# A fused attention and two-layer feed-forward kernel: the order of gates and blocks at two stage changes

## The chip, the cores and the metric

The kernel runs on one core of a Trainium2 chip. The metric is the device time of one execution in microseconds (us); of several runs the median counts. Five engines work side by side, each through its own queue in order: PE (matrix products; its weight loads are shown as PEld), DVE (vector), ACT (scalar functions), POOL (GpSimd) and SP, which issues the transfers.

## What is computed

```python
def reference(q, k, v, ...):
    x = attention(q, k, v, bias from w1, b1, w2)   # 2 x 576 rows, 8 heads of 64, float32
    x = x.reshape(1152, 512)
    h = x @ moe_w_in                               # layer 1: 512 -> 2048
    x = (h / (1 + exp(-1.702 * h))) @ moe_w_out    # gate of layer 1, 2048 -> 512
    h = x @ moe2_w_in                              # layer 2
    P = a0 + a1*h + a2*h**2 + a3*h**3
    Q = 1 + |b0|*|h| + |b1|*h**2
    return (P / (Q + 1e-6)) @ moe2_w_out
```

## The kernel before

**Precision.** Every large product is made from float32 numbers that are split into a high and a low part (hi, lo), as three products: hi by hi, weight lo by hi, weight hi by lo. ACT casts the high part, and POOL or DVE subtracts it from the number to get the low one.

**Attention** runs over 30 steps `s` (head pair, batch, block of 128 rows) and five more, s = 30 to 34, that drain it. The probabilities of step s - 3 are turned by PE (`transposes`, L295) into two PSUM banks `pt`, which ACT copies to SBUF as `PT` (`evacuate`, L354) in the next pass of the loop. Each bank must be copied before the next transposes write it. `values` (L370, L373) multiplies `PT` by v into `xt`, and `values_out` (L390, ACT) and `values_lo` (L395, DVE) make of it the input `xhi`, `xlo` of layer 1. In the passes s = 31, 32 and 33 the first three hidden blocks of layer 1 are computed beside that.

**The two layers.** The 1152 rows are three chunks of 384, and the 2048 hidden columns are 16 blocks `k`. One turn `n` of the main loop issues on PE one hidden block (`hidden`, L483, 12 products into one of two PSUM buffers `hps`) and usually one output block (`out1`, L564, of layer 1, 12 products; `out2`, L571, of layer 2, 9 products) into the banks `acc`. In this text H0 to H47 are the hidden blocks of layer 1, G0, G1, ... those of layer 2; o0 to o47 and p0, p1, ... are the output blocks of the two layers.

- The gate of layer 1 (`gelu`) is a sigmoid on ACT (L501), a product on DVE (L502, which is the last reader of `hps`), and `parts`: a cast on ACT (L492) and a subtraction on POOL (L495). `ghi` and `glo` have two buffers each.
- The gate of layer 2 (`rational`) is a pipeline over three turns. In one turn it issues for the newest block G(m): L527 to L529 on ACT, L541 and L545 on DVE (L545 is the last reader of `hps`), L542 and L544 on POOL; for G(m-1): L524 and L525 on ACT, L535 and L536 on DVE; for G(m-2): L521 on ACT, L531 on DVE and `parts`. L524 needs another function table than the sigmoid, so an ACT_TABLE_LOAD stands where ACT changes between them. Up to turn 51, L521 and L525 write one PSUM buffer, `es`; from turn 52 L521 writes the bank `acc3`.
- Chunk 2 of layer 2 comes first. The last output blocks of layer 1 belong to chunk 0: after o47, DVE adds the four `acc` banks to earlier partial sums (`input2_sum`, L824). The first output block p0 of layer 2 writes the same banks, so it waits for L824. ACT and POOL split those sums (L829, L830) in the four turns after it.
- Weights come as 64-bit numbers, one half block per transfer. `conv` turns them into float32: L445 on ACT, L446, L451 and L461 on DVE; `split` then makes the two parts (L471 ACT, L472 POOL). L446 writes the PSUM tile `top` while `M.second` is false, and the SBUF tile `tmp` when it is true. A half block of layer 2 goes to where the same block of layer 1 lay, once that is read for the last time. Halves still missing at the change of layer are converted one in every second turn, between the instructions of the rational gate. The last is the output weight of block 15, needed by p15 in turn 67.

Everything is written in the order in which it is issued; no scheduler moves anything. Before the change the order of the blocks at the change of layer is a list:

```python
    turn = [*range(N1 - 2), N1, N1 - 2, N1 + 1, N1 - 1, *range(N1 + 2, len(seq))]   # N1 = 48
    pos = {m: n for n, m in enumerate(turn)}
    ...
        while todo and n >= (pos[todo[0]] + L1 if todo[0] < N1 else todo[0] + L2):  # L1, L2 = 2, 4
```

So G0 stands ahead of H46 and G1 ahead of H47, and an output block is issued two turns (layer 1) or four (layer 2) after its hidden block.

Of the kernel before, what the change touches and what calls it, by code (L numbers as in the profile page):

```python
# [17 lines left out]
NF = 16  # L18
# [4 lines left out]
L1, L2 = 2, 4  # L23
# [551 lines left out]
def attention_moe_moe(tc, t):  # L575
    nc = tc.nc
    new = tc.alloc_tile_pool
    A, M = Attention(tc, t), Moe(tc, t)
# [44 lines left out]
    def beat():  # L623
        i = beats[0]
        beats[0] += 1
        if i >= 41:
            return
        if i == 2:
            A.bias_setup2()
        if 3 <= i < 39:  # L630
            A.bias_out(A.rows[i - 3])
        if 2 <= i < 38:
            A.bias_matmul(A.rows[i - 2])
        if i < 36:
            A.bias_hidden(A.rows[i])
        if i in (10, 17, 24, 31, 39):
            A.bias_load(0, QORDER[(10, 17, 24, 31, 39).index(i)])
        if i in (3, 10):
            A.new_parts(i // 10)
            A.q_high(i // 10)  # L640
        if i in (5, 8, 12, 15):
            A.q_low(i // 10, 0 if i in (8, 15) else 320, 320 if i in (8, 15) else 640)
        if i in (6, 13):
            A.k_high(i // 10)
        if i in (7, 14):
            A.k_low(i // 10)
        if i in (21, 26, 34):
            A.load_v((21, 26, 34).index(i))
        if i in (14, 16, 18, 22):
            A.load_qk(2, (14, 16, 18, 22).index(i))  # L650
        if i == 7:
            nc.vector.memset(small[:, 2:3], -1.5)
            nc.scalar.activation(out=M.pb, in_=ab[:, 4:6], func=AF.Abs)

    n = len(A.steps)
    nj = [0]

    def conv(now=True):
        M.conv(nj[0])
        nj[0] += 1  # L660
        if now:
            M.split()

    pv, hq, due = [], [], []
    A.pv = pv
    g, nh = {}, 0
    for s in range(n + TLAG + 2):
        prep = []
        while s <= 10 and beats[0] < FIRST[s]:
            beat()  # L670
        if s < n:
            hp, b, qc = A.steps[s]
            pb = 2 * hp + b
            i = QORDER.index(qc)
            A.tails(s - TLAG)
            A.scores(s)

            prep = [(2, s - 3)] if s <= 10 else [(s // 5 + 1, s % 5)] if s >= 15 else [(3, s - 10)]
            if s == 11:
                prep.insert(0, (3, 0))  # L680
            if prep[0][0] > 7:
                prep = []
            for x, part in prep:
                if part == 0:
                    A.new_parts(x)
        else:
            A.values_out()
            A.values_lo()
            A.tails(s - TLAG)
        if s == n:  # L690
            A.ps.release()
            M.hs = new(name="hs", bufs=1, space=PSUM, side="right", reuse_waits="tile")
            op.release()
            gp = M.gp = new(name="gate", bufs=1, side="right", reuse_waits="tile")
            mid = new(name="wmid", bufs=1, side="right", reuse_waits="tile")
            for k in range(NEARLY, NMID):
                M.W[k] = mid.tile([128, 4, 512], F32R, name=f"w{k}")
        if s - n in (2, 3):
            g[len(g)] = M.gelu(hq.pop(0))
        if s < 10:  # L700
            beat()
        if s == 10:
            A.xp.release()
            A.xp = new(name="xt", bufs=1, space=PSUM, reuse_waits="tile")
        for piece in (('ea', 'to', 'qh', 'eb', 'ql', 'kh', 'xa', 'su', 'cv', 'pv', 'tr', 'xb', 'no', 'vo', 'kl', 'vl') if s < 12 else ('ea', 'vo', 'to', 'pv', 'eb', 'qh', 'ql', 'kh', 'xa', 'tr', 'xb', 'su', 'no', 'vl', 'cv', 'kl')):
            if piece == 'ea':
                A.evacuate(0)
            elif piece == 'eb':
                A.evacuate(1)
            elif piece == 'su':  # L710
                A.sums(s - 1)
            elif piece == 'to':
                A.tails_out(s - TLAG)
            elif piece == 'vo':
                A.values_out()
            elif piece == 'vl':
                A.values_lo()
            elif piece == 'qh':
                for x, part in prep:
                    if part == 0:  # L720
                        A.q_high(x)
            elif piece == 'kh':
                for x, part in prep:
                    if part == 1:
                        A.k_high(x)
            elif piece == 'kl':
                for x, part in prep:
                    if part == 2:
                        A.k_low(x)
            elif piece == 'ql':  # L730
                for x, part in prep:
                    if part in (1, 3):
                        A.q_low(x, 320 if part == 1 else 0, 640 if part == 1 else 320)
            elif piece == 'xa':
                A.exps(s, 0)
            elif piece == 'xb':
                A.exps(s, 1)
            elif piece == 'no':
                A.normalise(s - 1)
            elif piece == 'tr':  # L740
                A.transposes(s - TLAG)
            elif piece == 'pv':
                for _ in range(5 if s >= n or len(pv) > 5 else 2 if pv and pv[0][1] == 0 else 3):
                    if pv and s >= 10:
                        A.values(*pv.pop(0))
                if s == n + TLAG + 1 and 1:
                    A.values_out()
                    A.values_lo()
            elif piece == 'cv':
                for _ in range(n - s in (3, 7, 12, 17, 21) if s < n else (0, 3, 0, 2, 0)[s - n]):  # L750
                    conv()
        if s < n:
            if s == 10:
                A.load_qk(3)

            if s:
                h, o, c = A.steps[s - 1]
                if h < 3 and (h, 1 - o, c) in A.steps[:s - 1]:
                    due.append((h + 1, c))
            while due and (s in (3, 4) or s >= 10):  # L760
                A.bias_load(*due.pop(0))
            if pb > 1 and i == 1:
                A.load_qk(pb + 2)
            if pb > 2 and i == 1:
                A.load_v(pb)
        if s == 10:
            bp.release()
        if s == n - 25:
            pp.release()
            rp = M.rp = new(name="raw", bufs=1, side="right", reuse_waits="tile")  # L770
            wp = new(name="wearly", bufs=1, side="right", reuse_waits="tile")
            for k in range(NEARLY):
                M.W[k] = wp.tile([128, 4, 512], F32R, name=f"w{k}")

        if s == n - 24:
            for j in range(3):
                M.fetch(j)
        if s - n in (1, 2, 3):
            hq.append(M.hidden(0, nh))
            nh += 1  # L780
# [20 lines left out]
    seq = [(0, c, k) for c in range(NC) for k in range(HF)]  # L801
    seq += [(0, c, k) for c in range(NC)[::-1] for k in range(HF, NF)]
    seq += [(1, c, k) for c in range(NC)[::-1] for k in range(NF)]
    N1 = NC * NF

    turn = [*range(N1 - 2), N1, N1 - 2, N1 + 1, N1 - 1, *range(N1 + 2, len(seq))]
    pos = {m: n for n, m in enumerate(turn)}
    freed = {k: max(pos[n] for n in range(N1) if seq[n][2] == k) for k in range(NF)}
    acc, ng, later, hr = {}, len(g), [], []
    gq = list(range(N1, len(seq)))  # L810
    todo = list(range(len(seq)))
# [18 lines left out]
        nc.gpsimd.tensor_tensor(out=lo, in0=p, in1=hi.bitcast(F32), op=ALU.subtract)  # L830

    for n in range(nh, len(seq) + L2):
        l, c, k = seq[turn[n]] if n < len(seq) else (2, 0, 0)
        M.second = n >= N1 - 2
        if l < 2:
            (hr if l else hq).append(M.hidden(c, k))
        fs = []
        for i in range(2):
            j = nj[0]
            if j < 33:  # L840
                go = i == 0 or n < 6
            elif j < 65:
                go = freed[M.order[j - 1][1]] + L1 * M.order[j - 1][2] < n
                go = go and (n < N1 and (i == 0 or n >= 40 and n % 2 == 0) or n >= N1 + 2 and n % 2 == 0 and i == 0)
            else:
                go = False
            if go and n >= N1:
                fs = M.convs(j)
                nj[0] += 1
            elif go:  # L850
                conv(False)
            if n < N1:
                M.split()
            if i == 0 and n <= len(seq) and ng <= turn[n - 1] < N1:
                g[turn[n - 1]] = M.gelu(hq.pop(0))
        if hr or n >= len(seq):
            r = M.rational(hr.pop(0) if hr else None, n < N1 + 4, fs)
            if r:
# [1 line left out]
        M.split()  # L860
        if later:
            input2_parts()
        while todo and n >= (pos[todo[0]] + L1 if todo[0] < N1 else todo[0] + L2):
            m = todo.pop(0)
            l, c, k = seq[m]
            first = k == 0 or l == 0 and c < 2 and k == HF
# [104 lines left out]
```

## Time and profile before

| | us |
|---|---|
| median of 3 runs (612.31 to 613.96) | 613.54 |
| the profiled execution, its own time | 613.64 |
| its span, first to last instruction | 611.6 |
| PE busy in the span | 575.5 |
| ACT busy | 444.4 |
| DVE busy | 430.0 |
| POOL busy | 393.1 |

The span has four stages: attention with its bias (0 to about 190), layer 1 (to about 400), layer 2 (to about 607), and the last outputs. The table counts work over all of them; a change at a stage boundary is judged by the rows around that boundary. Times in the rows are us from the start of the span. A timeline row gives the start, the duration of the group, engine, line, operation, output and inputs, the count, and in brackets the idle time of the engine just before it with the instruction that ended it.

### The profile page before, as it was taken

Reading aid. Unit: us, or ns where it says so; the run is one execution under the profiler, and the core shown is the slowest. Engines: PE = TensorE matmul, PEld = TensorE weight load, DVE = VectorE, ACT = ScalarE, POOL = GpSimd, SP = SyncE. Lnnn points to the kernel's source line nnn. Section 1 sums busy time; section 2 is a strip of 40 time slices with the busy share of each in tenths; the row PEclk is TensorE's granted clock in tenths of the full one; section 3 lists DMA queues with packets and bytes.
Section 4 is the critical chain, followed back from the end, with each engine's and each line's share of the span. In section 5 each row is a group of like instructions: output and inputs, shape, how many; then the busy total and the mean of one; then the engine's idle time right before and its main releaser. Section 6 shows DMA issues by size and latency. Waiting matters only on the chain. (4 is left out here: it accounts for less than half of the span.)

```text
span 611.6 us, 11023 instructions
## 1 busy us (share of the span) xinstructions
PE 575.5 (94%) x3805; PEld 482.6 (79%) x3805; DVE 430.0 (70%) x922; ACT 444.4 (73%) x928; POOL 393.1 (64%) x466
## 2 busy tenths in 40 slices
PE   6987999999987999999999999979999999999997
PEld 2243466666656899999999999968998998998995
DVE  7989765888874886657554528868998666666663
ACT  7978777898885665546444526688999888788783
POOL 5967656788763675546553536957998566565563
PEclk9989999999998999999999999997999999999999
DMA  5788853826214563525432314511200100001001
GB/s 173 209 265 280 232 211 104 299 83 243 61 36 138 168 195 124 170 75 167 138 112 95 104 36 138 158 48 35 71 0 2 51 2 1 1 1 52 2 1 51
DMA packets 23912, 66.25 MB, mean 108 GB/s; under 512 B 2481, under 2 KB 3377, under 8 KB 23857
## 3 DMA queue, kind: packets, MB, share of 16 engines
q1 hardware_dynamic: 23712, 65.43, 33.8%
q8 instruction: 30, 0.49, 0.3%
q14 instruction: 26, 0.20, 0.1%
q10 hardware_dynamic: 144, 0.13, 0.1%
HBM read 52.30 MB, written 13.25 MB: 107 GB/s over the span
## 5 line engine op out<-in xcount | busy, mean ns | idle before, releaser
L483 PE MATMUL hps<-xhi,w 128*128 128x384 f32 x768 | 152.6, 340 | 2.3 <-DVE part L545 1.0
L483 PEld LDWEIGHTS hps<-xhi,w 128*128 128x128 f32 x768 | 137.9, 190 | 8.0 <-DVE sg L502 1.5
L472 POOL TENSOR_TENSOR w<-tmp,w 128x512 fp32r<-128x512 f32 x64 | 86.7, 1354 | 37.4 <-ACT w L471 31.6
L495 POOL TENSOR_TENSOR glo<-sg,ghi 128x384 fp32r<-128x384 f32 x48 | 49.2, 1025 | 57.7 <-PE acc L564 37.4
L483 PE MATMUL hps<-xlo,w 128*128 128x384 f32 x384 | 82.6, 336 | 0.0
L571 PE MATMUL acc<-w,ghi 128*128 128x512 f32 x288 | 77.2, 398 | 3.3 <-DVE part L824 3.3
L253 POOL TENSOR_SCALAR p<-p,mn 128x512 f32<-128x512 f32 x72 | 55.2, 777 | 37.8 <-ACT p L240 26.3
L564 PE MATMUL acc<-ghi,w 128*128 128x384 f32 x384 | 78.3, 334 | 0.0
L240 ACT ACTIVATE p<-p,mn 128x576 f32<-128x576 f32 x72 | 55.6, 773 | 20.1 <-DVE mn L236 18.1
L483 PEld LDWEIGHTS hps<-xlo,w 128*128 128x128 f32 x384 | 68.5, 189 | 0.0
L564 PEld LDWEIGHTS acc<-ghi,w 128*128 128x128 f32 x384 | 67.6, 188 | 0.0
L542 POOL TENSOR_SCALAR ra<-ra,small 128x384 f32<-128x384 f32 x48 | 28.2, 588 | 56.3 <-ACT ra L527 56.3
L571 PEld LDWEIGHTS acc<-w,ghi 128*128 128x128 f32 x288 | 54.1, 190 | 12.4 <-issue 3.6
L502 DVE TENSOR_TENSOR sg<-hps,sg 128x384 f32<-128x384 f32 x48 | 26.8, 558 | 52.0 <-ACT sg L501 52.0
L236 DVE CUSTOM_DVE_ANT_0 p<-wide,bt 128x576 f32<-128x576 f32 x72 | 52.3, 751 | 2.3 <-PE wide L215 2.1
L492 ACT CAST ghi<-sg 128x384 fp32r<-128x384 f32 x48 | 24.8, 517 | 38.7 <-DVE sg L502 19.9
L544 POOL TENSOR_TENSOR ra<-ra,part 128x384 f32<-128x384 f32 x48 | 49.8, 1038 | 4.0
L445 ACT ACTIVATE up<-raw 128x512 int32<-128x512 uint32 x59 | 37.9, 642 | 19.9 <-DVE tmp L461 15.9
L215 PE MATMUL wide<-k,q 64*128 64x288 f32 (+1 forms) x432 | 45.9, 313 | 2.5 <-ACT st L142 2.0
L564 PE MATMUL acc<-glo,w 128*128 128x384 f32 x192 | 45.0, 334 | 0.0
L501 ACT ACTIVATE sg<-hps 128x384 f32<-128x384 f32 x48 | 23.4, 488 | 28.3 <-PE hps L483 28.3
L571 PE MATMUL acc<-w,glo 128*128 128x512 f32 x144 | 43.1, 397 | 0.0
(112 smaller groups left out, 1187.6 us busy)
## 6 DMA issues: line engine op xcount, KB each, us to landing
raw<-win SPq DMA_DIRECT2D x32, 512.0 KB, 3.5
raw<-wout SPq DMA_DIRECT2D x32, 512.0 KB, 3.5
bias_all<-st SPq DMA_DIRECT2D x36, 295.5 KB, 3.8
bt<-bias_all SPq DMA_DIRECT2D x16, 576.0 KB, 6.0
qk<-qk SPq DMA_DIRECT2D x7, 608.0 KB, 5.3
v<-v SPq DMA_DIRECT2D x8, 320.0 KB, 5.0
out<-o SPq DMA_DIRECT2D x8, 256.0 KB, 2.2
bt<-bias_all SPq DMA_DIRECT2D x8, 144.0 KB, 3.4
```

Of the source, the lines that this page charges most:

```text
L215: nc.tensor.matmul(ps[:, half, 0:288], q[p, x, 128 * qc:128 * qc + 128], k[p, y, 288 * half:288 * half + 288], start=(i == 0), stop=(i == ...
L236: nc.vector.tensor_tensor_reduce(out=pv.rearrange("p (x j) -> p x j", x=2), in0=ps[:, :, 0:288], in1=self.bt[qc][:, a, :].rearrange("p (x ...
L240: nc.scalar.activation(out=pv, in_=pv, func=AF.Exp, bias=mn[:, a:a + 1], scale=-1.0, accum_out=mn[:, 2 + a:3 + a])
L253: nc.gpsimd.tensor_scalar(out=p[:, a, 0:512], in0=p[:, a, 0:512], scalar1=r, scalar2=1.0, op0=ALU.mult, op1=ALU.mult)
L445: nc.scalar.activation(out=self.up[j].bitcast(I32), in_=lo, func=AF.Copy, scale=2.0 ** -29)
L472: nc.gpsimd.tensor_tensor(out=w[:, 2 * o + 1, :], in0=val, in1=w[:, 2 * o, :].bitcast(F32), op=ALU.subtract)
L483: nc.tensor.matmul(ps[:, 0:CH], w[:, wi, 128 * d:128 * d + 128], xx[:, d, :], start=(i == 0 and d == 0), stop=(i == 2 and d == 3))
L495: nc.gpsimd.tensor_tensor(out=glo[:], in0=g, in1=ghi[:].bitcast(F32), op=ALU.subtract)
L542: nc.gpsimd.tensor_scalar(out=t0[0][:], in0=t0[0][:], scalar1=self.pb[:, 1:2], scalar2=1.000001, op0=ALU.mult, op1=ALU.add)
L544: nc.gpsimd.tensor_tensor(out=t0[0][:], in0=t0[0][:], in1=t0[1][:], op=ALU.add)
L564: nc.tensor.matmul(acc[e][:, 0:CH], w[:, wi, 128 * e:128 * e + 128], g[gi][:], start=(first and i == 0), stop=(last and i == 2))
L571: nc.tensor.matmul(acc[e][:], g[gi][:, 128 * e:128 * e + 128], w[:, wi, :], start=(first and i == 0), stop=(last and i == 2))
```

## The change

Two edits. In the drain of attention, the gate of a layer-1 block is issued at the place `cv`, behind that pass's copies of probabilities (L354), and no longer ahead of them. At the change of layer the list is gone: all hidden blocks of layer 1 come first, then those of layer 2; `due` gives the turn of each output block, with o46 in turn 49 and o47 in turn 51. With it, `M.second` turns true at turn 48, where it did at 46, and the conversions of the second layer's weights resume at turn 52, where they did at 50.

```diff
-        if s - n in (2, 3):
-            g[len(g)] = M.gelu(hq.pop(0))
         if s < 10:
             beat()
...
             elif piece == 'cv':
+                if s - n in (2, 3):
+                    g[len(g)] = M.gelu(hq.pop(0))
                 for _ in range(n - s in (3, 7, 12, 17, 21) if s < n else (0, 3, 0, 2, 0)[s - n]):
                     conv()
...
-    turn = [*range(N1 - 2), N1, N1 - 2, N1 + 1, N1 - 1, *range(N1 + 2, len(seq))]
-    pos = {m: n for n, m in enumerate(turn)}
-    freed = {k: max(pos[n] for n in range(N1) if seq[n][2] == k) for k in range(NF)}
+
+    due = [m + L1 + (m - N1 + 3 if m > N1 - 3 else 0) if m < N1 else m + L2 for m in range(len(seq))]
+    freed = {k: max(due[n] - L1 for n in range(N1) if seq[n][2] == k) for k in range(NF)}
...
-        l, c, k = seq[turn[n]] if n < len(seq) else (2, 0, 0)
-        M.second = n >= N1 - 2
+        l, c, k = seq[n] if n < len(seq) else (2, 0, 0)
+        M.second = l > 0
...
-                go = go and (n < N1 and (i == 0 or n >= 40 and n % 2 == 0) or n >= N1 + 2 and n % 2 == 0 and i == 0)
+                go = go and (n < N1 and (i == 0 or n >= 40 and n % 2 == 0) or n >= N1 + 4 and n % 2 == 0 and i == 0)
...
-            if i == 0 and n <= len(seq) and ng <= turn[n - 1] < N1:
-                g[turn[n - 1]] = M.gelu(hq.pop(0))
+            if i == 0 and ng <= n - 1 < N1:
+                g[n - 1] = M.gelu(hq.pop(0))
...
-        while todo and n >= (pos[todo[0]] + L1 if todo[0] < N1 else todo[0] + L2):
+        while todo and n >= due[todo[0]]:
```

What moves on the engines is shown at three places. First ACT at the end of attention, passes s = 32 to 33; `PT` is the copy of the turned probabilities, `sg` and `ghi` the gates of H0 and H1, `xhi` the input of layer 1:

```order
+L354 COPY PT<-pt 128x8x64 x2
 L501 ACT_TABLE_LOAD
 L501 ACTIVATE sg<-hps 128x384
 L492 CAST ghi<-sg 128x384
-L354 COPY PT<-pt 128x8x64 x2
 L390 CAST xhi_103<-xt 128x192
 L390 CAST xhi_105<-xt 128x64 x2
-L501 ACTIVATE sg<-hps 128x384
-L492 CAST ghi<-sg 128x384
-L354 COPY PT<-pt 128x8x64 x2
+L354 COPY PT<-pt 128x8x64 x2
+L501 ACTIVATE sg<-hps 128x384
```

Each pair of copies moves ahead of one gate; the number of instructions stays the same.

Second the change of layer, on PE and on ACT. On PE, `hps<-xhi_101` with w_2977 and w_2978 is H46 and H47; with `xhi_105`, w_1324 and w_1325 it is G0 and G1; `acc` with w_2975 and w_2976 is o44 and o45. Before:

```order
L483 MATMUL hps<-xhi_105,w_1324 128x384 x8
L483 MATMUL hps<-xlo_106,w_1324 128x384 x4
L564 MATMUL acc<-ghi,w_2975 128x384 x8
L564 MATMUL acc<-glo,w_2975 128x384 x4
L483 MATMUL hps<-xhi_101,w_2977 128x384 x8
L483 MATMUL hps<-xlo_102,w_2977 128x384 x4
L564 MATMUL acc<-ghi,w_2976 128x384 x8
L564 MATMUL acc<-glo,w_2976 128x384 x4
L483 MATMUL hps<-xhi_105,w_1325 128x384 x8
L483 MATMUL hps<-xlo_106,w_1325 128x384 x4
L483 MATMUL hps<-xhi_101,w_2978 128x384 x8
L483 MATMUL hps<-xlo_102,w_2978 128x384 x4
```

Now:

```order
L483 MATMUL hps<-xhi_101,w_2977 128x384 x8
L483 MATMUL hps<-xlo_102,w_2977 128x384 x4
L564 MATMUL acc<-ghi,w_2975 128x384 x8
L564 MATMUL acc<-glo,w_2975 128x384 x4
L483 MATMUL hps<-xhi_101,w_2978 128x384 x8
L483 MATMUL hps<-xlo_102,w_2978 128x384 x4
L564 MATMUL acc<-ghi,w_2976 128x384 x8
L564 MATMUL acc<-glo,w_2976 128x384 x4
L483 MATMUL hps<-xhi_105,w_1324 128x384 x8
L483 MATMUL hps<-xlo_106,w_1324 128x384 x4
L483 MATMUL hps<-xhi_105,w_1325 128x384 x8
L483 MATMUL hps<-xlo_106,w_1325 128x384 x4
```

PE's sequence was G0 o44 H46 o45 G1 H47 o46 and is H46 o44 H47 o45 G0 G1 o46; from there on it is the same as before: G2, G3, o47, G4, p0. On ACT, in the same place, the gate of H47 (the second L501 here) comes ahead of the whole rational gate, and of three table loads one is left:

```order
-L527 ACTIVATE ra<-hps 128x384
-L528 ACTIVATE part_2980<-hps,cst 128x384
-L529 ACTIVATE part_2980<-hps,cst 128x384
 L445 ACTIVATE up<-raw 128x512
 L471 CAST w_2973<-tmp 128x512
 L501 ACTIVATE sg<-hps 128x384
 L492 CAST ghi<-sg 128x384
+L501 ACTIVATE sg<-hps 128x384
+L492 CAST ghi<-sg 128x384
+L527 ACTIVATE ra<-hps 128x384
+L528 ACTIVATE part_2980<-hps,cst 128x384
+L529 ACTIVATE part_2980<-hps,cst 128x384
```

Third POOL at the last weight half of layer 2, w_2978 (block 15); each group L542, L544, L495 is one turn:

```order
 L542 TENSOR_SCALAR ra<-ra,small 128x384
 L544 TENSOR_TENSOR ra<-ra,part_2980 128x384
-L495 TENSOR_TENSOR glo<-ra,ghi 128x384
+L495 TENSOR_TENSOR glo<-part_2980,ghi 128x384
 L472 TENSOR_TENSOR w_2978<-tmp,w_2978 128x512
-L542 TENSOR_SCALAR ra<-ra,small 128x384
-L544 TENSOR_TENSOR ra<-ra,part_2980 128x384
-L495 TENSOR_TENSOR glo<-part_2980,ghi 128x384
-L542 TENSOR_SCALAR ra<-ra,small 128x384
-L544 TENSOR_TENSOR ra<-ra,part_2980 128x384
-L495 TENSOR_TENSOR glo<-part_2980,ghi 128x384
```

Its split moves two turns later, from turn 64 to turn 66.

## Rows read from the trace of the kernel before

**Rows 1.** Windows: busy time of each engine, granted clock (PEclk), DMA share, GB/s.

```profile
260.00:280.00 20.00, 20.00 (x118) 20.00 (x117) 12.12 (x21) 10.65 (x21) 11.00 (x10) 1.00 0.36 106
410.00:420.00 10.00, 6.74 (x21) 5.58 (x20) 8.29 (x17) 6.85 (x15) 5.82 (x7) 0.66 0.18 54
```

**Rows 2.** Timeline of PE, end of attention and start of layer 1.

```profile
193.19 0.27 PE L295 MATMUL pt<-cst,p 64*128 64x64 f32 x1 [3.09 <-ACT PT L354]
...
194.32 2.50 PE L483 MATMUL hps<-xhi,w 128*128 128x384 f32 x8
...
197.90 1.74 PE L483 MATMUL hps<-xhi,w 128*128 128x384 f32 x8
...
222.16 1.66 PE L483 MATMUL hps<-xhi,w 128*128 128x384 f32 x8
```

**Rows 3.** Timeline of ACT, end of attention.

```profile
189.73 1.28 ACT L501 ACT_TABLE_LOAD   x1
...
192.14 0.51 ACT L492 CAST ghi<-sg 128x384 fp32r<-128x384 f32 x1 [0.62 <-DVE sg L502]
192.56 1.07 ACT L354 COPY PT<-pt 128x512 f32<-128x512 f32 x2
193.51 0.56 ACT L390 CAST xhi<-xt 128x192 fp32r<-128x192 f32 x3
198.14 0.49 ACT L501 ACTIVATE sg<-hps 128x384 f32<-128x384 f32 x1 [4.06 <-PE hps L483]
```

**Rows 4.** Timeline of DVE, start of layer 1.

```profile
198.66 0.56 DVE L502 TENSOR_TENSOR sg<-hps,sg 128x384 f32<-128x384 f32 x1 [3.94 <-ACT sg L501]
...
216.54 0.56 DVE L502 TENSOR_TENSOR sg<-hps,sg 128x384 f32<-128x384 f32 x1 [0.24 <-ACT sg L501]
...
221.55 0.56 DVE L502 TENSOR_TENSOR sg<-hps,sg 128x384 f32<-128x384 f32 x1 [0.24 <-ACT sg L501]
```

**Rows 5.** Timeline of PE, change of layer.

```profile
385.54 1.55 PE L483 MATMUL hps<-xhi,w 128*128 128x384 f32 x8
...
414.18 1.19 PE L571 MATMUL acc<-w,ghi 128*128 128x512 f32 x2 [3.26 <-DVE part L824]
...
423.26 1.57 PE L483 MATMUL hps<-xhi,w 128*128 128x384 f32 x8
...
427.44 1.57 PE L483 MATMUL hps<-xhi,w 128*128 128x384 f32 x8
```

**Rows 6.** Timeline of ACT, change of layer.

```profile
396.20 1.28 ACT L524 ACT_TABLE_LOAD   x1
397.50 0.53 ACT L524 ACTIVATE part<-ra 128x384 f32<-128x384 f32 x1
...
410.82 0.47 ACT L527 ACTIVATE ra<-hps 128x384 f32<-128x384 f32 x1
...
415.46 0.59 ACT L521 ACTIVATE sq<-ra,small 128x384 f32<-128x384 f32 x1 [2.73 <-DVE part L824]
```

**Rows 7.** Timeline of DVE, change of layer.

```profile
413.48 1.95 DVE L824 TENSOR_TENSOR part<-acc,part 128x384 f32<-128x384 f32 x4
```

**Rows 8.** Timeline of ACT, first chunk of layer 2: L527 of five blocks.

```profile
439.29 0.48 ACT L527 ACTIVATE ra<-hps 128x384 f32<-128x384 f32 x1
...
442.94 0.48 ACT L527 ACTIVATE ra<-hps 128x384 f32<-128x384 f32 x1
...
447.34 0.48 ACT L527 ACTIVATE ra<-hps 128x384 f32<-128x384 f32 x1
...
463.46 0.48 ACT L527 ACTIVATE ra<-hps 128x384 f32<-128x384 f32 x1
...
467.43 0.49 ACT L527 ACTIVATE ra<-hps 128x384 f32<-128x384 f32 x1 [0.31 <-PE hps L483]
```

**Rows 9.** Timeline of POOL, the split of the last weight half, turn 64.

```profile
470.65 1.29 POOL L472 TENSOR_TENSOR w<-tmp,w 128x512 fp32r<-128x512 f32 x1
```

**Rows 10.** Timeline of PE, p15 in turn 67.

```profile
479.79 1.09 PE L571 MATMUL acc<-w,ghi 128*128 128x512 f32 x4
```

## The prediction

> **What bounds the kernel now.** I read the windows first. From about 230 to 376 us PE is busy in the whole of each window at full clock, as in the first row of [rows 1]: there, time can only move if PE's stage starts earlier or ends later. The second row is the exception in the two layers: at the change of layer PE worked 6.74 of 10 us, at a mean clock of 0.66. So two places remain, and I read the timelines of the engines around each.
>
> At the end of attention PE stands 3.09 us before the last transposes, waiting for ACT's copies of `PT` [rows 2]. ACT has them queued behind the first gate: table load at 189.73, sigmoid, a wait for DVE, the cast at 192.14, and only then the copies at 192.56 [rows 3]. H1 after it takes from 194.32 to 197.90 [rows 2], 3.6 us for a block that takes 2.1 later on, so the standstill costs clock too.
>
> At the change of layer the longest standstill is 3.26 us [rows 5]. It ends with L824 on DVE, which frees the output banks [rows 7]. From p0 at 414.18 to G6 at 423.26 three blocks take 9.08 us; two blocks take 4.18 at full clock (423.26 to 427.44) [rows 5], so three should take 6.27. That is 2.8 us lost to the half clock.
>
> **The change part by part.**
>
> *Gate behind copies.* Nothing is added or taken away on any engine; two pairs of copies and two gates change places on ACT. The first copies come where the table load stood, 189.73 instead of 192.56: 2.83 earlier, and PE's transposes with them, from 193.19 to about 190.4. The load follows at 189.73 + 0.95 = 190.7 (0.95 is what the copies take until the next instruction starts, 192.56 to 193.51). From load to cast it is 2.41 as now (189.73 to 192.14), so the cast comes at 193.1. After it come `xhi` (0.42 behind the cast, then about 0.5) and the second copies (0.95), and the sigmoid of H1 starts at about 195.0 instead of 198.14 [rows 2, 3]. H1 itself is done by then: transposes done at 191.5 (194.32 less 2.83), plus 2.1, or 3.6 if the clock is low. So ACT and DVE gain 3.1 us, and PE could gain up to 5.
>
> What decides is who sets the pace next. From the gate at 198.66 on, DVE converts weights between the gates, two halves a turn at first, and a turn takes 5.0 us on it (216.54 to 221.55) against 4.2 on PE. The hidden block at 222.16 starts the moment the gate of the block two before it is done (221.55 + 0.56) [rows 2, 4]. PE's extra lead is therefore spent in front of `hps`, and what reaches 222 is DVE's gain, **3.1 us**. The bounds are 0, if this chain does not start earlier, and PE's 5. The stage after it is full on PE [rows 1], so it carries the gain whole.
>
> *Order at the change of layer.* PE's work is the same. G0 moves from 385.54 to four blocks later, 385.54 + 4 x 2.09 = 393.9, ending at 396.0 [rows 5]. Before that, ACT and DVE have only gates and conversions of layer 1, and two table loads drop out. ACT can take G0 up as soon as it is done, with H47's gate behind it.
>
> From there the length of the chain to L824 decides. It runs through L527 of G0, G1, G2 and G3, one step each. The trace of before has no such steps without gates of layer 1 in them; the nearest are those of the first chunk, where ACT is nearly packed too: 439.29 to 442.94, 3.65 without a conversion, and 442.94 to 447.34, 4.40 with one [rows 8]. No conversion stands in turns 48 to 51 now, so I take 3.65, with a little for the `es` buffer that L521 and L525 share: 3.7. The one table load left lies in the first step, which has no L521 and no `parts` of an older block; it costs 1.30 (396.20 to 397.50, the next instruction starting at once) [rows 6], little more than what it stands in for. Three steps are 11.1, so L527 of G3 comes at 407.2. From L527 to L824 it was 2.66 (410.82 to 413.48), from L824 to p0 0.70 [rows 5 to 7]: L824 at 409.9 and p0 at 410.6 instead of 414.18, **3.6 earlier**. With steps of 4.40 it would be 1.5 earlier. PE's wait for p0 becomes about 1.6 us.
>
> The Trainium skill ("ScalarE: Activation LUTs", What ACT_TABLE_LOAD costs) gives a switch as 1.283 us and a drain of 1.38. The row shows the load alone, 1.28. By the page the one load that still stands on each of the two chains would cost 1.4 us more, and the total gain would come out near 4.2 us; the row decides.
>
> *Clock, and what is late next.* If 1.6 us of rest leaves the clock up, PE runs p0 to G6 2.8 us faster than before, and would be 6.4 ahead. But ACT is not: L521 in turn 52 waits for the last L824 [rows 6], moves by 3.6 with it, and ACT is nearly packed from there until it waits for PE at 467.43 [rows 8]. L545 stands right ahead of L824 and so ends some 2.7 behind L527; it frees `hps` for the hidden block two later. For G9 that is 439.29 - 3.6 + 2.7 = 438.4, while PE could start G11 at 423.26 + 5 x 4.18 - 6.4 = 437.8 [rows 5, 8]. So PE is held by 0.6, and about 5.7 is left.
>
> The conversions resumed two turns later cost more. The last half of block 15 is split in turn 66, and p15 in turn 67 reads its low part in its second product, about 480.0 [rows 10]. In turn 64 the split ended at 470.65 + 1.29 = 471.94, 4.5 behind L527 of G16 at 467.43 [rows 8, 9]. Now L527 of G15 comes 3.6 earlier, 459.9, that of G18 three steps later (3.65 + 4.40 + 3.65 = 11.7), 471.6, and the split ends at 476.1. So p15 gains **3.9 us** however far PE is ahead, and PE waits about 1.8 us in front of it. If the clock falls as before, ACT waits for PE instead, and p15 comes about 0.3 later than PE's own 3.6 allow: 3.3. The clock hardly matters, because the weight takes back what it gives. After p15 no conversion is left, and the rest of the kernel is as before.
>
> The sum: 3.1 + 3.9 = 7.0, from the profiled execution's own 613.64, which is 0.1 above the median: **606.6 us**.
>
> **The rivals.**
>
> - *The last weight is not late.* If ACT's turns 60 to 66 run ahead, PE keeps 5.7: 613.64 - 3.1 - 5.7 = 604.8. Against it: three steps, one with a conversion, are in the rows.
> - *The gate's move is hidden.* DVE and ACT reach the block at 222.16 no earlier, for instance because the raw weights for the conversions land no earlier: then only 3.9 is gained, 609.7. For it: PE's gain there is already limited by DVE. Against: DVE sat 3.94 us idle before 198.66 for nothing but the sigmoid [rows 4].
> - *Only the gate's move counts.* The chain to L824 runs with long steps, and the late weight takes the rest: 613.64 - 3.1 = 610.5.
> - *Neither reaches the end*: both waits are replaced by others just as long: 613.5.
> - *Slower, by the late start of layer 2.* G0 now ends on PE 8.4 us later. From its end before (387.6) to L824 it took 25.9 us. If that length were the chain's own and not that of the gates in it, L824 would come at 396.0 + 25.9 = 421.9, 8.4 late; with the gate's gain the kernel takes 618.9. It decides from a chain over 13.9 + 3.6 + 3.1 = 20.6 us. Against it: two table loads (2.6 us), two gates and a conversion lay in those 25.9 and are gone from the chain.
>
> **How the numbers follow.** Forecast 0.57; last weight in time 0.10; gate hidden 0.10; only the gate 0.10; neither 0.07; slower 0.06. A measurement tells about 0.3%, 1.8 us, from no change. The first four are faster by more: 0.87; neither is the same: 0.07; the last is slower: 0.06. The range takes in the second (604.8, less 0.6 for PE's wait for `hps`, should it not arise) and the third and fourth (610.5): 604.2 to 610.5.
>
> **What would show it.** Right: PE's wait of 3.09 before L295 is under 0.5, and H1 takes 2.1; the block at 222.16 starts near 219.0; p0 starts 6.7 us earlier, near 407.5, behind a standstill of 1 to 2 us; one table load remains between the layers; and p15 waits one to two us for POOL's L472. Wrong: L824 less than 4 us earlier than 413.48, a new wait of PE for `hps` or `ghi` before o46, or a start of the block at 222.16 that has not moved.

## The result and the profile after

| | before | after |
|---|---|---|
| median, us | 613.34 (4 runs, 612.31 to 613.96) | 606.99 (4 runs, 605.67 to 607.56) |
| the profiled execution, its own time | 613.64 | 607.07 |
| its span | 611.6 | 605.2 |

The ratio is 0.990 with a 95% interval of 0.9878 to 0.9921. Forecast were 606.6 us and a gain of 7.0; the medians give 6.35. A second measurement, on one chip with two experiments, gives 613.06 and 606.06, a gain of 7.0 (ratio 0.989, 0.987 to 0.9911).

To see where the time came from I lay the traces of both kernels on one another at an instruction that no edit moves: the last L288 of attention, on PE (pass 32). It starts at 186.79 before and at 187.84 after. So the attention of the second execution ran 1.05 us later, and clock times from the start of the span can't be compared directly. Below, PE's rows around this place, first one of before, then those of after:

```profile
186.79 0.27 PE L288 MATMUL tl<-cst,ptl 128*128 128x128 f32 x1
```

```profile
187.84 0.27 PE L288 MATMUL tl<-cst,ptl 128*128 128x128 f32 x1
...
191.21 0.27 PE L295 MATMUL pt<-cst,p 64*128 64x64 f32 x1
...
192.33 1.68 PE L483 MATMUL hps<-xhi,w 128*128 128x384 f32 x8
...
194.54 1.55 PE L483 MATMUL hps<-xhi,w 128*128 128x384 f32 x8
...
214.64 1.68 PE L483 MATMUL hps<-xhi,w 128*128 128x384 f32 x8 [0.56 <-DVE sg L502]
...
219.65 1.67 PE L483 MATMUL hps<-xhi,w 128*128 128x384 f32 x8 [0.55 <-DVE sg L502]
```

The wait of 3.09 in front of L295 [rows 2] is gone: the row has no bracket any more. H1 takes 2.2 us (192.33 to 194.54) where it took 3.6. The block that stood at 222.16, H7, is 31.81 behind L288 (219.65 - 187.84); it was 35.37 behind. That is 3.56 us. It starts when L502 on DVE is done, as before; PE now stands 0.55 in front of it.

The timeline of ACT in the same place shows the new order, copies first, then the load and the gates:

```profile
190.57 1.07 ACT L354 COPY PT<-pt 128x512 f32<-128x512 f32 x2
191.66 1.28 ACT L501 ACT_TABLE_LOAD   x1
192.95 0.49 ACT L501 ACTIVATE sg<-hps 128x384 f32<-128x384 f32 x1
194.07 0.51 ACT L492 CAST ghi<-sg 128x384 fp32r<-128x384 f32 x1 [0.62 <-DVE sg L502]
194.49 0.54 ACT L390 CAST xhi<-xt 128x192 fp32r<-128x192 f32 x3
194.90 1.10 ACT L354 COPY PT<-pt 128x512 f32<-128x512 f32 x2
195.86 0.54 ACT L501 ACTIVATE sg<-hps 128x384 f32<-128x384 f32 x1
```

The sigmoid of H1 (195.86) follows the copies at once; before, it waited 4.06 for PE [rows 3].

At the change of layer these are PE's rows (G0, p0, G6, G9), and behind them the windows there:

```profile
391.36 1.55 PE L483 MATMUL hps<-xhi,w 128*128 128x384 f32 x8
...
408.30 0.70 PE L571 MATMUL acc<-w,ghi 128*128 128x512 f32 x2 [1.49 <-DVE part L824]
...
414.64 1.57 PE L483 MATMUL hps<-xhi,w 128*128 128x384 f32 x8
...
427.62 1.69 PE L483 MATMUL hps<-xhi,w 128*128 128x384 f32 x8 [0.22 <-DVE part L545]
```

```profile
400.00:410.00 10.00, 8.25 (x44) 7.65 (x45) 7.50 (x15) 6.31 (x14) 5.15 (x6) 1.00 0.01 2
410.00:420.00 10.00, 10.00 (x52) 9.10 (x51) 8.83 (x15) 9.55 (x21) 8.12 (x9) 1.00 0.16 52
```

The wait for p0 is 1.49 instead of 3.26 [rows 5], the granted clock stays at 1.00 (the level of 2.4 GHz) where the mean was 0.66 [rows 1], and p0 to G6 takes 6.34 instead of 9.08. The chain that ends this wait, on ACT (L527 of G0, G1, G2, G3, and the one table load left) and DVE:

```profile
393.64 0.49 ACT L527 ACTIVATE ra<-hps 128x384 f32<-128x384 f32 x1 [0.65 <-PE hps L483]
...
395.18 1.28 ACT L524 ACT_TABLE_LOAD   x1
396.48 0.52 ACT L524 ACTIVATE part<-ra 128x384 f32<-128x384 f32 x1
...
397.46 0.47 ACT L527 ACTIVATE ra<-hps 128x384 f32<-128x384 f32 x1
...
401.20 0.48 ACT L527 ACTIVATE ra<-hps 128x384 f32<-128x384 f32 x1
...
404.94 0.48 ACT L527 ACTIVATE ra<-hps 128x384 f32<-128x384 f32 x1
```

```profile
407.60 1.95 DVE L824 TENSOR_TENSOR part<-acc,part 128x384 f32<-128x384 f32 x4
```

And the place that the prediction named as late next, the last weight half (POOL) and p15 (PE):

```profile
472.13 1.26 POOL L472 TENSOR_TENSOR w<-tmp,w 128x512 fp32r<-128x512 f32 x1
```

```profile
473.45 0.96 PE L571 MATMUL acc<-w,ghi 128*128 128x512 f32 x3 [1.17 <-POOL w L472]
```

By such rows the span falls into distances, which I give for every kernel that was run, in us. Each is the difference of two starts on PE: L288, H7, p0, the second product of p15, and the end of the span. Where the second product has no row of its own, it is 0.23 behind the first, a quarter of the 0.92 that four products took.

| kernel | L288 to H7 | H7 to p0 | p0 to p15 | p15 to the end | sum |
|---|---|---|---|---|---|
| before | 35.37 | 192.02 | 65.84 | 131.58 | 424.81 |
| after | 31.81 | 188.65 | 65.15 | 131.75 | 417.36 |
| only the gate moved | 31.83 | 192.00 | 65.64 | 131.64 | 421.11 |
| only the order changed | 33.87 | 188.58 | 65.06 | 131.74 | 419.25 |
| after, weight in time | 31.81 | 188.61 | 64.39 | 131.57 | 416.38 |
| after, outputs close | 31.82 | 188.71 | 63.97 | 131.69 | 416.19 |
| after, buffer as before | 31.78 | 189.31 | 65.17 | 131.72 | 417.98 |
| after, close and in time | 31.81 | 190.06 | 63.26 | 131.59 | 416.72 |
| after, conversions from turn 50 | 31.78 | 190.04 | 64.65 | 131.57 | 418.04 |
| after, a conversion moved | 30.23 | 188.66 | 65.15 | 131.68 | 415.72 |
| three edits, outputs close | 30.23 | 188.76 | 63.25 | 131.58 | 413.82 |
| two edits, outputs apart | 30.25 | 188.65 | 64.38 | 131.59 | 414.87 |
| after, once more | 31.82 | 188.63 | 65.09 | 131.70 | 417.24 |

From L288 on the changed kernel is 7.45 shorter: 3.56 up to H7, 3.37 up to p0, 0.69 up to p15, less 0.17 at the end. Less the 1.05 by which its attention was later, that is 6.4, the difference of the spans. Each row of the table is one execution, and may lie on either side of its kernel's median.

### The profile page after: what moved, and what is told of

Its sections match the earlier page's. It is cut to its first block, busy times and chain, and to the rows that moved or that the text cites. A ratio compares the mean times of both kernels' runs of the same rounds, so it can differ in the third digit from the quotient of the medians.

```text
span 605.2 us, 11019 instructions
## 1 busy us (share of the span) xinstructions
PE 571.9 (95%) x3805; PEld 478.5 (79%) x3805; DVE 427.2 (71%) x922; ACT 440.6 (73%) x926; POOL 392.4 (65%) x466
## 4 chain that ended last, share of the span: by engine, by line
PE 48%; ACT 8%; DVE 5%; POOL 4%; issue 1%; DVEq 0%; POOLq 0%; ACTq 0%
PE hps L483 24%; PE acc L564 13%; PE acc L571 11%; POOL ra L544 2%; DVE tmp L461 1%; POOL w L472 1%; ACT es L525 1%; ACT part L524 1%; ACT part L528 1%; ACT up L445 1%; ACT ra L527 1%; ACT part L529 1%; POOL glo L495 1%; DVE part L824 1%; ACT w L471 1%
## 5 line engine op out<-in xcount | busy, mean ns | idle before, releaser
L483 PEld LDWEIGHTS hps<-xhi,w 128*128 128x128 f32 x768 | 135.5, 188 | 8.9 <-DVE sg L502 3.1
L472 POOL TENSOR_TENSOR w<-tmp,w 128x512 fp32r<-128x512 f32 x64 | 85.9, 1343 | 37.6 <-ACT w L471 31.9
L495 POOL TENSOR_TENSOR glo<-sg,ghi 128x384 fp32r<-128x384 f32 x48 | 49.0, 1021 | 52.8 <-PE acc L564 37.3
L542 POOL TENSOR_SCALAR ra<-ra,small 128x384 f32<-128x384 f32 x48 | 28.4, 592 | 53.9 <-ACT ra L527 53.7
L502 DVE TENSOR_TENSOR sg<-hps,sg 128x384 f32<-128x384 f32 x48 | 26.8, 558 | 50.6 <-ACT sg L501 50.6
L544 POOL TENSOR_TENSOR ra<-ra,part 128x384 f32<-128x384 f32 x48 | 50.0, 1042 | 4.0
L501 ACT ACTIVATE sg<-hps 128x384 f32<-128x384 f32 x48 | 23.6, 492 | 24.3 <-PE hps L483 24.3
```

Source lines behind the costliest of these rows:

```text
L472: nc.gpsimd.tensor_tensor(out=w[:, 2 * o + 1, :], in0=val, in1=w[:, 2 * o, :].bitcast(F32), op=ALU.subtract)
L483: nc.tensor.matmul(ps[:, 0:CH], w[:, wi, 128 * d:128 * d + 128], xx[:, d, :], start=(i == 0 and d == 0), stop=(i == 2 and d == 3))
L495: nc.gpsimd.tensor_tensor(out=glo[:], in0=g, in1=ghi[:].bitcast(F32), op=ALU.subtract)
L542: nc.gpsimd.tensor_scalar(out=t0[0][:], in0=t0[0][:], scalar1=self.pb[:, 1:2], scalar2=1.000001, op0=ALU.mult, op1=ALU.add)
L544: nc.gpsimd.tensor_tensor(out=t0[0][:], in0=t0[0][:], in1=t0[1][:], op=ALU.add)
```

## The experiments

The theory is the prediction's: (1) the gate ahead of the copies cost about 3 us, and DVE's conversions cap what its move brings; (2) at the change of layer the chain from G0 to L824 sets p0, and it got shorter and started in time; (3) behind p0, buffers and the late last weight give some of it back. The rivals: one of the two parts does all of it; the shared buffer or the place of o46 and o47, which came along, does it, and not the order of the blocks.

### The two parts alone

The kernel before with the gate behind the copies, and nothing else:

```diff
-        if s - n in (2, 3):
-            g[len(g)] = M.gelu(hq.pop(0))
...
             elif piece == 'cv':
+                if s - n in (2, 3):
+                    g[len(g)] = M.gelu(hq.pop(0))
```

> The kernel before with the gate behind the copies alone. My theory: DVE's and ACT's lead of 3.1 us carries through layer 1, about 610.2 us; PE's wait ahead of the last transposes under 0.5 us, and the change of layer as in the kernel before, with its wait of 3.3 us for L824 and the half clock after it. Rival, the gate's move is hidden behind the conversions: 613.3 us, with the block that stood at 222.16 where it was against the end of attention.

Measured: 609.57 us, ratio 0.9944 (0.9922 to 0.9965). At the change of layer the trace is that of before, with wait and low clock:

```profile
410.42 1.19 PE L571 MATMUL acc<-w,ghi 128*128 128x512 f32 x2 [3.26 <-DVE part L824]
```

The other way round, the changed kernel with the gate ahead of the copies:

```diff
+        if s - n in (2, 3):
+            g[len(g)] = M.gelu(hq.pop(0))
...
             elif piece == 'cv':
-                if s - n in (2, 3):
-                    g[len(g)] = M.gelu(hq.pop(0))
```

> The changed kernel with the gate ahead of the copies again. My theory: the order alone gains 3.9 us, about 609.4 us; PE waits 3.1 us ahead of the last transposes as before, about 1.5 us ahead of p0 with the clock up, and about 1.2 us in p15 for the last weight half. Rival, the order gains only together with the gate or not at all: 612.5 us or more.

Measured: 610.27 us (10 runs), ratio 0.996 (0.9941 to 0.9978). The parts add up: 0.56% and 0.40% make 0.96%, and both together measure 1.0%. So neither part does it alone. By these medians the gate alone brings 3.29 us, near the 3.1 forecast, and the order alone 2.59 (1.35 to 3.62), less than the 3.9. The execution profiled here took 609.18, 1.09 under its median, and that of before 613.64, so the distances give the order more. PE's timeline at the end of attention has the wait again, but not the low clock:

```profile
194.26 0.27 PE L295 MATMUL pt<-cst,p 64*128 64x64 f32 x1 [2.99 <-ACT PT L354]
...
195.38 1.68 PE L483 MATMUL hps<-xhi,w 128*128 128x384 f32 x8
...
197.60 1.55 PE L483 MATMUL hps<-xhi,w 128*128 128x384 f32 x8
```

H1 takes 2.2 us here, and H7 comes 33.87 behind L288; in before, with H1 at 3.6, it was 35.37. So of the 3.56 that the gate's move brings in the traces, 1.5 is a fall of the clock which follows that wait in one execution and not in another.

### What sets the pace up to H7

The prediction held that DVE, with two conversions a turn, spends PE's lead. The changed kernel with one conversion fewer in pass 33, that of H1's gate, and all later ones a place later:

```diff
-                for _ in range(n - s in (3, 7, 12, 17, 21) if s < n else (0, 3, 0, 2, 0)[s - n]):
+                for _ in range(n - s in (3, 7, 12, 17, 21) if s < n else (0, 3, 0, 1, 0)[s - n]):
```

> Changed kernel with one conversion fewer at the last pass of attention (1 instead of 2 in the pass in which H0's gate runs), all later ones a place later. Theory (DVE sets the pace in turns 4 to 7): DVE has about 1.1 us less to do before H7, PE's waits of 0.56 in front of H6 and H7 go, H7 starts about 1.0 earlier after the attention, and the kernel takes about 606.0. Rival: what holds H7 is the gate's own chain (sigmoid, DVE, ACT), not the conversions: 607.0. Other rival: a weight of layer 2 comes a place later and is waited for at p15: 607.5.

Measured: 604.56 us, ratio 0.9877 (0.9857 to 0.9897). PE's rows of H6 and H7 (L288 is at 188.88 in this trace):

```profile
214.74 1.55 PE L483 MATMUL hps<-xhi,w 128*128 128x384 f32 x8
...
219.11 1.68 PE L483 MATMUL hps<-xhi,w 128*128 128x384 f32 x8
```

Both waits are gone, and H7 comes 30.23 behind L288 instead of 31.81: 1.58 earlier, more than the 1.0 expected. DVE's gates still follow each other at 5.0 us, and the wait for the last weight in front of p15 is still there (1.15). So DVE did set the pace, and by the distances the gain is kept to the end (415.72 against 417.36). The interval of the ratio still overlaps with the changed kernel's.

### What came along with the order

The shared buffer: `M.second` turns true in turn 46 again, as before the change.

```diff
-        M.second = l > 0
+        M.second = n >= N1 - 2
```

> Changed kernel, with the conversions of turns 46 and 47 writing the shared buffer again (as before the change they did one turn earlier than the turn of G0). Theory: in those two turns the gates of layer 1 then run later on ACT and DVE by a wait for a buffer, G0's L527 and with it p0 come about 1 us later, and the kernel takes about 608. Rival (only the order of the blocks matters, not the buffer): no change from the changed kernel, 607.0.

Measured: 607.17 us, ratio 0.992 (0.9902 to 0.9939), hardly apart from the changed kernel. In the trace G0 waits, and p0 is 0.66 later, where about 1 was expected. PE, then DVE and POOL where the time is lost:

```profile
390.47 1.66 PE L483 MATMUL hps<-xhi,w 128*128 128x384 f32 x8 [0.37 <-DVE sg L502]
```

```profile
381.72 0.42 DVE L446 TENSOR_SCALAR tmp<-raw 128x512 uint32<-128x512 uint32 x1
382.17 1.39 DVE L451 SCALAR_TENSOR_TENSOR tmp<-raw,tmp 128x512 uint32<-128x512 uint32 x1
...
384.81 1.16 DVE L446 TENSOR_SCALAR tmp<-raw 128x512 uint32<-128x512 uint32 x1
386.01 1.39 DVE L451 SCALAR_TENSOR_TENSOR tmp<-raw,tmp 128x512 uint32<-128x512 uint32 x1
...
388.87 0.69 DVE L451 SCALAR_TENSOR_TENSOR tmp<-raw,tmp 128x512 uint32<-128x512 uint32 x1
```

```profile
384.40 1.28 POOL L472 TENSOR_TENSOR w<-tmp,w 128x512 fp32r<-128x512 f32 x1
```

The same L446 on SBUF takes 0.42 where POOL is idle as it starts, and 1.16 where it starts inside POOL's L472; it ends 0.29 after that does (385.97 against 385.68). More is lost in L451 behind it, which now has both inputs in SBUF: 1.39 twice beside a busy POOL, 0.69 once beside an idle one. With `top` in PSUM, L446 and L451 take 0.69 each in every row of the changed kernel between 380 and 390. The Trainium skill ("SBUF — State Buffer", SBUF: two separate sides) says that GpSimd and VectorE, the latter in a mode that uses two ports or with two inputs in SBUF, lock a shared pair of ports for a whole instruction, so that the later one waits. The rows of L451, with its two inputs, agree; that L446 runs in such a mode is not shown here.

The conversions: resumed in turn 50 instead of 52, as before the change.

```diff
-                go = go and (n < N1 and (i == 0 or n >= 40 and n % 2 == 0) or n >= N1 + 4 and n % 2 == 0 and i == 0)
+                go = go and (n < N1 and (i == 0 or n >= 40 and n % 2 == 0) or n >= N1 + 2 and n % 2 == 0 and i == 0)
```

> Changed kernel with the conversions resumed in turn 50, as before the change, instead of 52. Theory: one step of the chain from G0 to L824 has a conversion in it and takes some 0.7 us longer, so p0 comes 0.7 later (wait for it about 2.2 instead of 1.49); the last weight half comes two turns earlier and the wait of 1.17 in front of p15 goes. Net about 606.6. Rival 1: the conversion hides in the chain, p0 is not later: 605.8. Rival 2: the wait for p0 passes 3 us, the clock falls, and most of 2 us is lost: 608.5.

Measured: 607.35 us, ratio 0.9914 (0.9897 to 0.9932). ACT's L527 of G2 and G3, and PE's p0:

```profile
400.41 0.47 ACT L527 ACTIVATE ra<-hps 128x384 f32<-128x384 f32 x1
...
405.52 0.47 ACT L527 ACTIVATE ra<-hps 128x384 f32<-128x384 f32 x1
```

```profile
408.88 0.70 PE L571 MATMUL acc<-w,ghi 128*128 128x512 f32 x2 [2.87 <-DVE part L824]
...
412.14 2.01 PE L483 MATMUL hps<-xhi,w 128*128 128x384 f32 x8
```

```profile
410.00:420.00 10.00, 10.00 (x44) 8.93 (x43) 8.51 (x16) 9.41 (x20) 7.55 (x8) 0.84 0.15 54
```

A step with a conversion takes 5.11 on ACT instead of 3.74. So p0 is 1.39 later, twice what was expected, the wait is 2.87, and the clock falls to a mean of 0.84: p0 to G6 takes 7.88 (408.88 to 416.76) instead of 6.34. The wait in front of p15 is gone, as was expected. By the distances the sum is 0.68 worse than after, and the medians can't tell the two apart. So the pause of the conversions is a real part of the shorter chain, and it is bought with the late weight. The order of the blocks without the pause and without the other buffer was not run. If their prices add, 0.66 and 1.39 of the 3.37 at p0 are theirs, and about 1.3 is left for the order itself.

### What takes back behind p0

One late conversion in turn 63, so that the last half is split a turn earlier:

```diff
-                go = go and (n < N1 and (i == 0 or n >= 40 and n % 2 == 0) or n >= N1 + 4 and n % 2 == 0 and i == 0)
+                go = go and (n < N1 and (i == 0 or n >= 40 and n % 2 == 0) or n >= N1 + 4 and (n % 2 == 0 or n == N1 + 15) and i == 0)
```

> The changed kernel with one more turn of conversion (63), so that the last weight half is split in turn 64 and not 66. My theory: the 1.17 us that PE waits in p15 for POOL's split go and nothing comes in its place: about 605.8 us. Rival: the extra conversion makes ACT 1.1 us later in turn 63, and the next hidden block or p15 waits as long: 607.0 us.

Measured: 605.50 us, ratio 0.9877 (0.9859 to 0.9894). The wait of 1.17 is gone; in its place PE waits for `hps` one turn earlier, at G18:

```profile
465.42 1.66 PE L483 MATMUL hps<-xhi,w 128*128 128x384 f32 x8 [0.29 <-DVE part L545]
```

In the changed kernel the turn that holds p15's wait takes 5.62 instead of 4.19, so the weight cost 1.43. Here two turns take 4.68 and 4.28, which is 0.58 too long. The distance from p0 to p15 shrinks by 0.76.

The last outputs of layer 1 close together, o46 and o47 two turns behind their hidden blocks:

```diff
-    due = [m + L1 + (m - N1 + 3 if m > N1 - 3 else 0) if m < N1 else m + L2 for m in range(len(seq))]
+    due = [m + L1 if m < N1 else m + L2 for m in range(len(seq))]
```

> The changed kernel with the last two outputs of layer 1 two turns behind their hidden blocks, as all others, and not three and four. My theory: L824 then comes behind the gate work of G1 instead of G3; p0 is held by G4 and its buffer and starts within 0.5 us of where it does now, but ACT no longer stands 2.7 us ahead of turn 52, so PE's waits for hps in turns 57 to 59 and most of the one in p15 go: about 605.5 us. Rival: the distance of the outputs is what carries the gain, since L824 and the splits behind it now stand in the chain of the rational gates: p0 2 us later or more, 609 us.

Measured: 606.16 us, ratio 0.989 (0.9866 to 0.9915). PE now stands in front of G4 and no longer in front of p0. PE, then ACT:

```profile
404.95 1.66 PE L483 MATMUL hps<-xhi,w 128*128 128x384 f32 x8 [2.20 <-DVE ra L545]
```

```profile
401.73 0.50 ACT L525 ACTIVATE es<-part 128x384 f32<-128x384 f32 x1 [2.35 <-DVE part L531]
...
426.78 0.48 ACT L527 ACTIVATE ra<-hps 128x384 f32<-128x384 f32 x1
```

p0 comes at the same distance (188.71 against 188.65). L824 now runs in the middle of the chain of gates instead of at its end, and there it costs as much: L525 on ACT waits for it, by way of L531, 2.35 us at 401.73. So where o47 is issued only decides in front of which block PE waits. But from then on L521 waits for nothing, where ACT stood 2.73 in turn 52. The four casts L829 fall two turns earlier, so that the last two of them are gone from the turns behind G6. ACT is level with the changed kernel up to G6 and 1.0 ahead at G8 (L527 at 426.78, 240.17 behind L288; in the changed kernel at 429.01, 241.17 behind it), and PE's waits for `hps` from G9 on are gone. The place in which the change put o46 and o47 is thus no part of its gain; it costs about a microsecond behind p0.

Both edits together:

> Changed kernel with the last outputs of layer 1 close together again and one of the late conversions a turn earlier, so that the last weight half is ready. Theory: the two gains of the single edits (0.8 for the outputs, 1.5 for the weight) overlap, since PE's wait for the weight shrank from 1.17 to 0.75 with the outputs close: about 605.0 with no wait for POOL's L472 in front of p15. Rival: they add up, 604.3. Other rival: the ACT engine, which then holds PE through hps, takes it all: 606.0.

Measured: 605.61 us, ratio 0.9887 (0.9871 to 0.9904). From p0 to p15 it takes 63.26. That is 1.89 less than after; the single edits gave 0.76 and 1.18, which make 1.94, so the two gains add up, where it was expected that they overlap. But up to p0 this trace has 190.06, because the clock fell at the wait in front of G4 (2.42 for the first row instead of 1.66, with the same wait). PE, then the window:

```profile
404.36 2.42 PE L483 MATMUL hps<-xhi,w 128*128 128x384 f32 x8 [2.20 <-DVE ra L545]
```

```profile
400.00:410.00 10.00, 7.80 (x34) 7.10 (x33) 7.77 (x16) 8.59 (x19) 7.31 (x9) 0.83 0.01 2
```

### All that helped

The three edits together (a conversion moved, the weight in time, the outputs close), the same with the outputs apart, and the changed kernel, on one chip with the kernel before at 613.06 (10 runs):

> Changed kernel with three edits: one conversion moved out of the last pass of attention, the last outputs of layer 1 close together, the last weight half a turn earlier. Theory (the three places are separate in time, so gains add, those of the last two as measured together): 606.9 less 1.6 (H7 earlier) less 1.3 = 604.0. Rival: a weight of layer 2, whose conversions all come a place later, is waited for, and the gain of 1.6 is lost: 605.6.

> As the kernel with three edits, but the last outputs of layer 1 further apart, as in the changed kernel. Theory (their place hardly matters once the weight is in time): 606.9 less 1.6 less 1.3 = 604.0, as the other. Rival (the outputs close together are the better order by the clock that stays up or ACT that runs ahead): 0.5 to 1 slower than the other.

> The changed kernel itself, beside the two others on one chip. If the differences between kernels are real and not those of chips: 607.0, that is 2.5 to 3 above the other two, and 0.990 of the kernel before.

| kernel | median, us | ratio to before, interval |
|---|---|---|
| three edits, outputs close | 602.60 | 0.9834 (0.981 to 0.9857) |
| two edits, outputs apart | 603.52 | 0.9852 (0.983 to 0.9875) |
| the changed kernel | 606.06 | 0.989 (0.987 to 0.9911) |

The first beats both kernels of this study: 3.5 us under the changed one, as its distances say (413.82 against 417.24 to 417.36), and more than the 2.9 (1.6 and 1.3) that was expected. Between 390 and 485 us of its trace one wait on PE is left that the profile names, the one in front of G4:

```profile
404.15 1.68 PE L483 MATMUL hps<-xhi,w 128*128 128x384 f32 x8 [2.21 <-DVE ra L545]
```

That the outputs close are better than apart is in the distances (63.25 against 64.38 from p0 to p15); by the medians it is 0.9 us with intervals that overlap.

## Why the prediction was right

Step by step, as the prediction put them; distances as above, so that the attention's 1.05 is out. It is still in the clock times that were named as signs: 219.65 for H7 (forecast 219.0) and 408.30 for p0 (407.5).

| step | forecast | measured, and how |
|---|---|---|
| sigmoid of H1 earlier | 3.1 | 3.33: 195.86 - 187.84 = 8.02, before 198.14 - 186.79 = 11.35 |
| H7 earlier, DVE's gain | 3.1 | 3.56 |
| G0 behind H7 | 171.7 (393.9 - 222.16) | 171.71 |
| the three steps of the chain | 3.7 each | 3.82, 3.74, 3.74 |
| L527 to L824, L824 to p0 | 2.66, 0.70 | 2.66, 0.70 |
| p0 earlier | 3.6 | 3.37 |
| PE's wait for p0 | 1.6 | 1.49 |
| clock stays up: p0 to G6 | 6.27 | 6.34 |
| PE held by `hps` | 0.6 | 0.67: G9 to G12 come 4.58, 4.34, 4.30 and 4.21 apart, not 4.19 |
| wait for the last weight | 1.8 | 1.17 in the row, 1.43 in the turn's length |
| p15 earlier, the order's part | 3.9 | 4.06: 3.37 + 0.69 |
| sum | 7.0 | 7.45 by the distances, 6.35 and 7.0 by medians |

**Gate.** The mechanism was right: PE's wait went, PE's lead was spent in front of `hps`, and DVE's gain reached H7. The conversion that was moved shows the cap by itself. The term was 0.46 too small. 0.23 of it is ACT, whose load, casts and copies took a little less than I had added up. The other part is DVE: in before it waits 0.38 for the last `xhi` between two conversions (L395 at 203.81); in after the same row, at 201.32, has no wait. That the size came so close is partly luck. It was read from an execution in which the clock fell at H1, and the fall is in the 198.14 from which the gain was counted; in the trace with the order alone, where the clock stays up, the gate is worth only 33.87 - 31.81 = 2.06. By the medians of its own run it is 3.29.

**Order.** In the trace the chain was right in its start, its steps and its end; ACT's waits in the steps are L525's for the buffer `es` (0.49 and 0.47 in ACT's timeline). By the medians the 3.9 is too large, 2.59 for the order alone, so the total is better confirmed than its split. The prediction gave the pause of the conversions no price of its own; undone, it costs p0 1.39. The step of 4.40 with a conversion, which served as the bound, was too short for this place (5.11).

**What is late next.** Both things named, `hps` and the weight of block 15, came; the first was sized well (0.6, 0.67), the second a little too large (1.8, 1.43). "The clock hardly matters, because the weight takes back what it gives" fits: p15 gained 0.69 behind p0, although PE ran the first blocks 2.74 faster (9.08 - 6.34). It was not tried, since no trace has both the late weight and a low clock behind p0.

**Rivals.** "The gate's move is hidden" and "only the gate's move counts" fall by the two parts alone, and "neither reaches the end" by the medians. "The last weight is not late" falls by the row of p15. "Slower, by the late start of layer 2" asked for a chain of over 20.6 us from G0's end to L824; it took 14.2 (407.60 less 393.44, where G1 starts). The rule of the Trainium skill ("ScalarE: Activation LUTs", What ACT_TABLE_LOAD costs) would have left, by the estimate in the prediction, a gain near 4.2. The trace disagrees with it at both loads: after 1.28 us the next ACTIVATE starts 0.02 or less behind (191.66 to 192.95, 395.18 to 396.48). The row of before (396.20 to 397.50) had shown the same [rows 6].

**What stays open.** The attention ends at different times: L288 starts between 185.98 and 188.88 in the 13 traces, though nothing ahead of it was edited. That is larger than most terms of the sum, and only medians take it out. The granted clock goes with part of it. In four traces it is 1.00 from 10 us to L288, which starts at 185.98 to 186.59. In the nine others it falls for a stretch (a mean of 0.93 or 0.97 from 10 to 60 us in eight, of 0.83 from 120 to 130 us in after), and L288 starts at 186.03 to 188.88, 187.31 on average. What lets it fall there was not tried.

## What to carry to other kernels

- When a gate stands in front of a copy that another engine waits for, price the gain by the engine that comes next, not by the wait that goes; here DVE capped a lead of 4.4 us on PE (H2 starts 6.70 behind L288, before 11.11) at 3.6, and a single conversion moved off DVE released another 1.6.
- At a change of stage, follow the one chain that frees the first shared buffer, step by step. Keep side work out of its steps, and look at once for what that side work is needed for, because that is late next (here a weight that is needed 15 turns on).
- Where two traces start a stage at different times, measure from an instruction that no edit moves.

## What was not expected of the hardware

**The clock after a wait of two to three microseconds is not the same each time.** After the waits of 1.5 for p0 (seven traces) the granted clock is 1.00 in the windows around. After 2.2 in front of G4 it stays at 1.00 in two traces and falls in the third, to a mean of 0.83. After 2.87 it falls. After about 3 in front of L295 it falls in before (3.09) and stays in the kernel with the order alone (2.99). After 3.26 it falls in both traces that have it. The clock shows in the times as well: of 30 runs of the kernel before, the 9 with a mean granted clock of 0.994 or more took 611.6 on average (610.95 to 612.10), the 21 with 0.992 or less 613.4 (612.15 to 615.75). How much of that is these waits is not shown, since the mean takes in the falls within attention. Part of what the change brings is that PE no longer has waits of such a length, and a single trace can show 1.5 us more or less for the fall at H1 alone (35.37 against 33.87).

**A DVE operation on SBUF can be faster or slower than on PSUM.** L446 takes 0.69 into PSUM, and into SBUF 0.42 beside an idle POOL or 1.16 beside a busy one. L451 takes 0.69 with one input in PSUM, and with both in SBUF 0.69 beside an idle POOL or 1.39 beside a busy one.
